# Plain float32 products on half of the array's rows, in a gated causal convolution kernel

## The chip, the core and the metric

One of the eight cores of a Trainium2 chip. The metric is the time of one execution on the device in microseconds (us). The engines: PE multiplies matrices (PEld is its loading of weights), DVE, ACT and POOL work element by element, SP starts transfers, and 16 DMA engines move data. PE writes to PSUM, which ACT and DVE read.

## What is computed

Eight batches of 4224 rows with 192 channels. First a dynamic convolution: each row has, for each of 8 heads of 24 channels, seven weights that a softmax makes, and sums its last seven rows with them. Then a gate: a causal convolution of five taps per channel, a sigmoid, times `x @ w_val`; and the product with `w_out`.

```python
w = np.exp(weight_gen - max) ; w = w / (w.sum(-1) + 1e-9)      # B, S, 8, 7
x = einsum('bshk,bskhg->bshg', w, last seven rows of x)         # dynamic convolution
gate_pre = sum(conv_w[k] * xp[:, k:k + S, :] for k in range(5)) # taps
gate = 1 / (1 + np.exp(-gate_pre))
out = (gate * (x @ w_val)) @ w_out
```

## The kernel before

**Tiling.** A block is 384 rows of one batch (`BLK`), a macro `i` is two blocks, and there are 44 macros. After the dynamic convolution channels lie in partitions and rows along the free dimension. The 192 channels are in two groups. Group A (g = 0) is 128 channels of a block, so a macro has two halves of it: tile `A`, 128 x (2 x 388). Group B (g = 1) is the other 64 channels: of a macro's first block in partitions 0 to 63 and of its second in 64 to 127, tile `B`, 128 x 388. The four extra columns are the history that the taps read.

**Stages of a macro**, each a function with the macro's index:

- `load_x`, `load_t`: SP's transfers of x and of the softmax weights (`tb`, from a scratch `zd` in DRAM that `Softmax.norm` writes through POOL's queue).
- `bank` (L355): four PSUM banks `pa` of 16 products each, in tiles of 32 columns of the array, four side by side.
- `evac` (L393, L395, L399): ACT copies the banks to `A`, `B` and a helper `S`; `moves` then fills holes in A and B from S with small transfers.
- `tap0` on ACT (L421, L424) and `tap` on DVE (L429), four each per group: the causal convolution into `aA` (128 x 768) and `aB` (128 x 384). `sigm` on ACT (L433).
- `split_a` (ACT L440, POOL L441) writes A as the sum of two parts of 12 bits, `hi` and `lo`. `split_b` and `gsplit` use `stack` (ACT L447, POOL L448): it puts the high part of block u's half into its own half of the partitions and the low part into the other half, into `q` (from B) and `g` (from the gated aB).
- `val`, three PSUM banks `pv`: kinds 0 and 1 are the first 128 output channels of block 0 and 1, five products each of float32r parts (L462); kind 2 is the other 64 output channels of both blocks in plain float32: one product on all of B (`wvd`, L464) and two with 64 columns each on A (`wvm`, L466).
- `gv` (DVE L473): gate times val, into aA or aB.
- `omm` (PE, L489, L490, L491): for 128 rows of a block, `g` times `woh`, `g` times `wob[u]` (both float32r, 256 columns), and aA times `woa` in plain float32 (192 columns). Two such chunks make a unit with one PSUM tile `po`, three units a macro.
- `oev` (ACT L499): copies `po` to `ot`; after the last unit SP sends ot to DRAM. The last macro sends each unit by itself.

**Order.** Every engine runs its instructions in the order of emission. `PLAN` gives each stage an offset in macros from its macro's index, and all stages are sorted by index plus offset: the dynamic convolution of macro i comes with val of macro i - 3 and out of macro i - 4 or i - 5. `Softmax` of later batches (max, sub, sum, recip, norm on DVE, exp on ACT) is spread between. PSUM: three tiles for `pa`, three for `pv`, two for `po`. Tiles of `A`, `B` and `S` hold two macros each and have two buffers.

Of the kernel before, what the change touches and what calls it, by code (L numbers as in the profile page):

```python
# [16 lines left out]
# The order in which the parts of the macros' work are emitted: each at the macro's index plus a number from here.  # L17
# [7 lines left out]
    splitB=2.7981,  # L25
    splitA=2.3938,
# [4 lines left out]
    gsplit=3.8257,  # L31
# [8 lines left out]
    spo=(2.2858, 3.439),  # L40
# [14 lines left out]
def tile_dynconv_gated_moe(  # L55
# [9 lines left out]
    nc = tc.nc  # L65
# [45 lines left out]
    wvh = const.tile([P, 2, P], FP32R, name="wvh")  # L111
    wvl = const.tile([P, 2, P], FP32R, name="wvl")
    wvb = [const.tile([P, P], FP32R, name=f"wvb{i}") for i in range(2)]
    wvm = const.tile([P, HD], FP32, name="wvm")
    wvd = const.tile([P, P], FP32, name="wvd")
    WO = 256
    woh = const.tile([P, WO], FP32R, name="woh")
    wob = [const.tile([P, WO], FP32R, name=f"wob{i}") for i in range(2)]
# [9 lines left out]
    woa = wf[:, 0, D:2 * D]  # L128

    # Channels live in two groups of partitions: group 0 is 128 channels of a block, group 1 the other 64,  # L130
    # those of a macro's first block in the lower half, of its second in the upper. Each quadrant holds 24
    # channels of one head and 8 of the last two heads.
# [11 lines left out]
    def order_weights():  # L144
        """Rows of the weights in DRAM in the order of their channels in the partitions."""
        d = wd.rearrange("(q r) n -> q r n", r=Q)
        for rows, c0, n in ((slice(0, C), 0, C), (slice(C, Q), c6, HC)):
            for j, w in enumerate((w_val, w_out)):
                nc.gpsimd.dma_start(out=d[:, rows, j * D:(j + 1) * D],
                                    in_=w[c0:c0 + n * NQ].rearrange("(q r) n -> q r n", r=n))  # L150
            nc.gpsimd.dma_start(out=cd.rearrange("j (q r) -> j q r", r=Q)[:, :, rows],
                                in_=conv_w[:, c0:c0 + n * NQ].rearrange("j (q r) -> j q r", r=n))
# [9 lines left out]
    def convert_weights(raw, cs, v, w):  # L162
        """raw, float64 in pairs of words (low, high), rounded to float32 in columns cs of wf."""
# [19 lines left out]
    def split_weights():  # L183
        """The columns of w_val in the order of the channels in the partitions: towards the first group as sums
        of two parts of 12 bits each, towards the second as they are. The second group's rows of w_out as such
        sums too."""
        units = []

        def runs(dst, src, q0, q1):
            """Quadrants q0 .. q1 - 1 of the columns: (dst, src) for both runs of channels in them."""  # L190
            d = dst.rearrange("p (a c) -> p a c", c=Q)
            return ((d[:, :, 0:C], src[:, C * q0:C * q1].rearrange("p (a c) -> p a c", c=C)),
                    (d[:, :, C:Q], src[:, c6 + HC * q0:c6 + HC * q1].rearrange("p (a c) -> p a c", c=HC)))
# [7 lines left out]
        for g in (1, 0):  # L201
            for (h, v), (l, _) in zip(runs(wvh[:, g], wf[:, g, 0:D], 0, 4), runs(wvl[:, g], wf[:, g, 0:D], 0, 4)):
                units.append(lambda h=h, v=v: nc.scalar.copy(out=h, in_=v))
                units.append(lambda h=h, l=l, v=v: nc.gpsimd.tensor_tensor(
                    out=l, in0=v, in1=h.bitcast(FP32), op=ALU.subtract))
            if g == 1:
                for b in range(2):
                    hs = slice(HD * b, HD * b + HD)
                    units.append(lambda b=b, hs=hs: nc.scalar.copy(out=wvb[b][hs], in_=wvl[hs, 1].bitcast(FP32)))
        s = wf[:, 1, D:2 * D]  # L210
        out_units = [lambda: nc.scalar.copy(out=woh[:, 0:D], in_=s)]
        for b in range(2):
            hs = slice(HD * b, HD * b + HD)
            out_units.append(lambda b=b, hs=hs: nc.gpsimd.tensor_tensor(
                out=wob[b][hs, 0:D], in0=s[hs], in1=woh[hs, 0:D].bitcast(FP32), op=ALU.subtract))
        return units, out_units
# [5 lines left out]
    class Softmax:  # L222
        """Softmax of rows r0 .. r0 + P * R - 1 of batch b: partition p takes R of them and the
        PAD after those, so that norm() can write for an input row its weights towards each output."""
# [72 lines left out]
    def where(i):  # L297
        """The two blocks of macro i as (batch, first row)."""
        return [((2 * i + u) // NBLK, (2 * i + u) % NBLK * BLK) for u in range(2)]

    def parts(i):
        """Runs of windows of macro i that lie at one distance: (batch, first row, window, windows)."""
# [37 lines left out]
    def bank(i, kind):  # L340
        """One PSUM bank of the dynamic convolution of macro i: block 0's or block 1's first four heads, the next
        two heads of both blocks, or the last two of both."""
# [24 lines left out]
    def pair(i, name, shape):  # L367
        """The tile of that name of macros i and i ^ 1."""
# [12 lines left out]
    def stir(n):  # L381
        """Work of no effect that keeps the clock of the tensor engine up while the first loads are on the way."""
# [18 lines left out]
    def moves(i, g):  # L401
        """Fill the holes of macros i - 1 and i, or of i alone where it is the only one left."""
# [32 lines left out]
    def split_a(i):  # L435
        s = st[i]
        a = s["A"][:, :, HALO:W]
        s["hi"] = work.tile([P, 2, BLK], FP32R, name="hi")
        s["lo"] = work.tile([P, 2, BLK], FP32R, name="lo")
        nc.scalar.copy(out=s["hi"], in_=a)  # L440
        nc.gpsimd.tensor_tensor(out=s["lo"], in0=a, in1=s["hi"].bitcast(FP32), op=ALU.subtract)  # L441

    def stack(src, dst, eng):
        """dst[:, u]: the high part of block u's half of src in its own half, the low part in the other."""
        for u in range(2):
            own, oth = slice(HD * u, HD * u + HD), slice(HD - HD * u, P - HD * u)
            nc.scalar.copy(out=dst[own, u], in_=src[own])  # L447
            eng.tensor_tensor(out=dst[oth, u], in0=src[own], in1=dst[own, u].bitcast(FP32), op=ALU.subtract)  # L448

    def split_b(i):  # L450
        s = st[i]
        s["q"] = work.tile([P, 2, BLK], FP32R, name="q")
        stack(s["B"][:, HALO:W], s["q"], nc.gpsimd)

    def val(i, k):
        s = st[i]
        pv = ps_v.tile([P, 512], FP32, name="pv")
        if k < 2:
            ops = [(wvh[:, 1], s["q"][:, k]), (wvb[k], s["q"][:, k]),
                   (wvh[:, 0], s["hi"][:, k]), (wvh[:, 0], s["lo"][:, k]), (wvl[:, 0], s["hi"][:, k])]  # L460
            for n, (w, r) in enumerate(ops):
                nc.tensor.matmul(out=pv[:, 0:BLK], lhsT=w, rhs=r, start=(n == 0), stop=(n == len(ops) - 1))  # L462
        else:
# [4 lines left out]
        s["pv", k] = pv  # L468
# [6 lines left out]
    def gsplit(i):  # L475
        s = st[i]
        s["g"] = work.tile([P, 2, BLK], FP32R, name="g")
        stack(s["aB"], s["g"], nc.gpsimd)

    CPB = BLK // CH  # L480
    OPU = 2

    def omm(i, k):
        s = st[i]
        po = ps_o.tile([P, OPU, WO], FP32, name="po")
        for v in range(OPU):
            u, j = divmod(k * OPU + v, CPB)
            cs = slice(CH * j, CH * j + CH)
            nc.tensor.matmul(out=po[:, v, :], lhsT=s["g"][:, u, cs], rhs=woh, start=True, stop=False)  # L489
            nc.tensor.matmul(out=po[:, v, :], lhsT=s["g"][:, u, cs], rhs=wob[u], start=False, stop=False)  # L490
            nc.tensor.matmul(out=po[:, v, 0:D], lhsT=s["aA"][:, u, cs], rhs=woa, start=False, stop=True)  # L491
        s["po", k] = po

    def oev(i, k):
# [4 lines left out]
        nc.scalar.copy(out=ot[:, k * OPU:(k + 1) * OPU, :], in_=s["po", k][:, :, 0:D])  # L499
        if i == NM - 1 and len(parts(i)) == 1:  # L500
            (b, r, _, _), = parts(i)
            r += k * OPU * CH
            nc.sync.dma_start(out=out[b, r:r + OPU * CH, :].rearrange("(t p) d -> p t d", p=P),
                              in_=ot[:, k * OPU:(k + 1) * OPU, :])
        elif (k + 1) * OPU == 2 * CPB:
# [4 lines left out]
            st[i] = {}  # L510

# [11 lines left out]
    for i in range(NM):  # L523
# [24 lines left out]
        at(sh + i + PLAN["splitB"], split_b, i)  # L548
        at(sh + i + PLAN["splitA"], split_a, i)
        for k, tt in zip((2, 0, 1), span(i, "val", 3)):  # L550
            at(sh + tt, val, i, k)
            at(sh + tt + PLAN["gvlag"], gv, i, k)
        at(sh + i + PLAN["gsplit"], gsplit, i)
        n = 2 * CPB // OPU
        for k, tt in enumerate(span(i, "out", n)):
# [24 lines left out]
    def clear(t, h, eng):  # L580
        """Zero half h of t."""
# [16 lines left out]
    for t in (*wvb, woh, *wob):  # L598
        nc.gpsimd.memset(t.bitcast(FP32), 0.0)
# [29 lines left out]
    sv, so = split_weights()  # L629
    for key, us in (("cvc", conv[2]), ("cvv", conv[0]), ("cvo", conv[1]), ("spv", sv), ("spo", so)):  # L630
# [3 lines left out]
    for _, _, f, a in sorted(ev, key=lambda e: e[:2]):  # L634
        f(*a)

# [25 lines left out]
```

## Time and profile before

| | |
|---|---|
| median of 3 runs | 649.92 us (647.55 to 651.01) |
| the profiled execution, its span | 650.0 us |
| mean granted TensorE clock | 0.971 |
| PE busy | 582.7 us (90%) |
| DVE busy | 601.7 us (93%) |
| ACT busy | 438.0 us (67%) |
| POOL busy | 376.6 us (58%) |
| DMA | 124.65 MB, mean 192 GB/s |

The span runs from the first to the last instruction of the profiled execution; its own time beside the span is not recorded apart, and the span stands within 0.1 us of the median. A row of a group reads: line, engine, operation, tile written <- tiles read, shapes, count, then busy us and mean ns of one, then the idle time of the engine before them and what ended most of it. A row of a timeline reads: start, length (to the end of the last where several are grouped), engine, line, operation, tiles, shapes, count. The length of a product includes its way through the array, so that successive ones overlap; what one costs in a dense run is read from start to start. L numbers are lines of the kernel before.

### The profile page before, as it was taken

How to read it: one execution, taken by the hardware profiler on the slowest of the kernel's cores; microseconds unless marked ns; L12 is line 12 of the kernel's file. 1: busy time of each engine (PE TensorE's matmuls, PEld its weight loads, DVE VectorE, ACT ScalarE, POOL GpSimd, SP SyncE). 2: the span in 40 equal slices, each digit the busy share in tenths (PEclk: the TensorE clock that was granted, in tenths of full speed). 3: DMA queues.
4: the chain of work that ended last, by engine and by line, in shares of the span. 5: the costliest groups of instructions: out<-in, count | busy, mean ns of one | idle time of the engine just before them, and what ended most of it. 6: DMA issues, size and time to landing. Idle time of an engine off the chain costs nothing.

```text
span 650.0 us, 18233 instructions
## 1 busy us (share of the span) xinstructions
PE 582.7 (90%) x7422; PEld 459.1 (71%) x7422; DVE 601.7 (93%) x653; ACT 438.0 (67%) x789; POOL 376.6 (58%) x292
## 2 busy tenths in 40 slices
PE   1356699998998999997999979998998999999976
PEld 0345477876787778775778857787876887788766
DVE  7867999999999899998999989998999998898994
ACT  4436396687748687586776768757966676667763
POOL 9154744774755645572665727556656556455673
PEclk9986799999999999999999999999998999999998
DMA  6879967997896968987598876997878658754313
GB/s 191 225 244 176 315 154 167 282 247 155 176 291 197 203 145 206 295 227 154 125 275 214 224 158 129 247 248 188 197 196 288 156 135 196 168 123 114 86 44 110
DMA packets 126914, 124.65 MB, mean 192 GB/s; under 512 B 9390, under 2 KB 121354, under 8 KB 126062
## 3 DMA queue, kind: packets, MB, share of 16 engines
q1 hardware_dynamic: 122970, 101.25, 65.3%
q0 software_dynamic: 3840, 22.23, 9.2%
q8 instruction: 59, 0.97, 0.7%
q14 instruction: 25, 0.20, 0.1%
q10 hardware_dynamic: 20, 0.01, 0.0%
HBM read 67.12 MB, written 50.36 MB: 181 GB/s over the span
## 4 chain that ended last, share of the span: by engine, by line
PE 45%; DVE 22%; DMA 19%; issue 4%; SPq 4%; ACT 4%; POOL 1%; DVEq 0%; ACTq 0%; POOLq 0%
PE pa L355 21%; DVE aA L429 9%; PE po L491 7%; DVE aB L429 6%; PE pv L462 5%; DMA tb<-zd 4%; DMA A<-S 4%; PE po L489 4%; DMA wt<-in_weight_gen_dram 3%; DMA zd<-zt 3%; PE pv L464 3%; PE pv L466 3%; PE po L490 3%; DVE zt L280 2%; SPq L334 2%
## 5 line engine op out<-in xcount | busy, mean ns | idle before, releaser
L355 PE MATMUL pa<-tb,xt 106*32 106x96 f32 (+1 forms) x5632 | 267.9, 357 | 37.4 <-ACT wt L260 22.2
L355 PEld LDWEIGHTS pa<-tb,xt 106*32 106x32 f32 x5632 | 206.7, 129 | 100.3 <-issue 63.1
L429 DVE SCALAR_TENSOR_TENSOR aA<-A,wf,aA 128x768 f32<-128x768 f32 x176 | 226.2, 1286 | 2.5 <-ACT aA L421 2.5
L429 DVE SCALAR_TENSOR_TENSOR aB<-B,wf,aB 128x384 f32<-128x384 f32 x176 | 193.5, 1100 | 0.0
L448 POOL TENSOR_TENSOR q<-B,q 64x384 fp32r<-64x384 f32 x88 | 112.3, 1277 | 99.6 <-ACT q L447 66.1
L441 POOL TENSOR_TENSOR lo<-A,hi 128x768 fp32r<-128x768 f32 x44 | 93.8, 2132 | 101.9 <-issue 35.2
L448 POOL TENSOR_TENSOR g<-aB,g 64x384 fp32r<-64x384 f32 x88 | 126.6, 1439 | 12.9 <-ACT g L447 6.4
L491 PE MATMUL po<-wf,aA 128*128 128x192 f32 x528 | 131.1, 330 | 2.1 <-DVE aA L473 2.1
L489 PE MATMUL po<-woh,g 128*128 128x256 f32 x264 | 98.9, 374 | 17.6 <-ACT ot L499 12.9
L491 PEld LDWEIGHTS po<-wf,aA 128*128 128x128 f32 x528 | 81.8, 191 | 2.6 <-DVE aA L473 2.5
L499 ACT COPY ot<-po 128x384 f32<-128x384 f32 x132 | 62.7, 476 | 25.2 <-PE po L491 24.2
L489 PEld LDWEIGHTS po<-woh,g 128*128 128x128 f32 x264 | 50.4, 191 | 35.4 <-ACT ot L499 15.2
L490 PE MATMUL po<-wob,g 128*128 128x256 f32 x264 | 74.4, 282 | 0.0
L393 ACT COPY A<-pa 128x388 f32<-128x388 f32 x88 | 41.2, 481 | 46.3 <-PE pa L355 27.5
L399 ACT COPY S<-pa 64x388 f32<-64x388 f32 x88 | 42.2, 479 | 29.9 <-PE pa L355 29.3
L473 DVE TENSOR_TENSOR aA<-pv,aA 128x384 f32<-128x384 f32 x88 | 48.1, 547 | 7.3 <-ACT aA L433 6.3
L490 PEld LDWEIGHTS po<-wob,g 128*128 128x128 f32 x264 | 50.6, 192 | 0.0
L421 ACT ACTIVATE aA<-A,wf 128x768 f32<-128x768 f32 x44 | 41.4, 941 | 12.7 <-DMA A<-S 9.1
L447 ACT CAST g<-aB 64x384 fp32r<-64x384 f32 x88 | 45.0, 512 | 4.6 <-DVE aB L473 2.7
L395 ACT COPY B<-pa 128x388 f32<-128x388 f32 x44 | 21.3, 483 | 38.0 <-DVE aB L429 17.8
L433 ACT ACTIVATE aA<-aA 128x768 f32<-128x768 f32 x44 | 37.4, 851 | 13.6 <-DVE aA L429 13.4
L447 ACT CAST q<-B 64x384 fp32r<-64x384 f32 x88 | 44.5, 506 | 1.1
(74 smaller groups left out, 711.0 us busy)
## 6 DMA issues: line engine op xcount, KB each, us to landing
xt<-in_x_dram SPq DMA_DIRECT2D x35, 672.0 KB
out_dram<-ot SPq DMA_DIRECT2D x39, 576.0 KB
tb<-zd SPq DMA_DIRECT2D x240, 88.0 KB
zd<-zt POOLq DMA_DIRECT2D x21, 968.0 KB, 6.8
wt<-in_weight_gen_dram SPq DMA_DIRECT2D x6, 1092.0 KB
A<-S SPq DMA_DIRECT2D x84, 48.5 KB
xt<-in_x_dram SPq DMA_DIRECT2D x5, 588.0 KB
out_dram<-ot SPq DMA_DIRECT2D x8, 288.0 KB
```

Of the source, the lines that this page charges most:

```text
L355: nc.tensor.matmul(out=pa[Q * c:Q * c + Q, at:at + n], lhsT=xb[0:KR, j, C * h:C * h + Q], rhs=t[0:KR, j, PAD + skip:PAD + skip + n, h], st ...
L399: nc.scalar.copy(out=t[:, 2 * m + u, :], in_=pa[HD * u:HD * u + HD, 0:W])
L421: nc.scalar.activation(out=s["aA"], in_=s["A"][:, :, 0:BLK], func=AF.Copy, scale=cw[:, 0, 0:1])
L429: nc.vector.scalar_tensor_tensor(out=a, in0=src, scalar=cw[:, g, j:j + 1], in1=a, op0=ALU.mult, op1=ALU.add)
L441: nc.gpsimd.tensor_tensor(out=s["lo"], in0=a, in1=s["hi"].bitcast(FP32), op=ALU.subtract)
L447: nc.scalar.copy(out=dst[own, u], in_=src[own])
L448: eng.tensor_tensor(out=dst[oth, u], in0=src[own], in1=dst[own, u].bitcast(FP32), op=ALU.subtract)
L473: nc.vector.tensor_tensor(out=a, in0=s["pv", k][:, 0:BLK], in1=a, op=ALU.mult)
L489: nc.tensor.matmul(out=po[:, v, :], lhsT=s["g"][:, u, cs], rhs=woh, start=True, stop=False)
L490: nc.tensor.matmul(out=po[:, v, :], lhsT=s["g"][:, u, cs], rhs=wob[u], start=False, stop=False)
L491: nc.tensor.matmul(out=po[:, v, 0:D], lhsT=s["aA"][:, u, cs], rhs=woa, start=False, stop=True)
L499: nc.scalar.copy(out=ot[:, k * OPU:(k + 1) * OPU, :], in_=s["po", k][:, :, 0:D])
```

## The change

The splits into 12-bit parts are gone (`split_a`, `split_b`, `gsplit`, `stack`, and the split weights `wvh`, `wvl`, `woh`). `val` of kinds 0 and 1 is emitted as one step: for each block a product on 64 rows of the array (`wvb[hs]` with block u's half of B, `tile_position=(64 * u, 0)`), then for each block one product on all rows (`wva` with A), all in plain float32. `omm` makes two units a macro: chunks 0 and 1 of both blocks, then chunk 2 of both. A unit takes two `po` tiles, one per block; its products of aA come first, then those of aB on half of the rows, alternating between the blocks. `oev` copies the two tiles apart. The last macro's output goes in one transfer. `probe`, emitted last, runs 64 products of no effect on a cleared tile `pz`, in tiles of 32 columns, and four float32r products. The other numbers of `PLAN` stay.

```diff
-    splitB=2.7981,
-    splitA=2.3938,
-    gsplit=3.8257,
-    spo=(2.2858, 3.439),
...
-        pv = ps_v.tile([P, 512], FP32, name="pv")
-        if k < 2:
-            ops = [(wvh[:, 1], s["q"][:, k]), (wvb[k], s["q"][:, k]),
-                   (wvh[:, 0], s["hi"][:, k]), (wvh[:, 0], s["lo"][:, k]), (wvl[:, 0], s["hi"][:, k])]
-            for n, (w, r) in enumerate(ops):
-                nc.tensor.matmul(out=pv[:, 0:BLK], lhsT=w, rhs=r, start=(n == 0), stop=(n == len(ops) - 1))
...
+        for k in kinds:
+            s["pv", k] = ps_v.tile([P, 512], FP32, name="pv")
...
+        for k in kinds:
+            hs = slice(HD * k, HD * k + HD)
+            nc.tensor.matmul(out=s["pv", k][:, 0:BLK], lhsT=wvb[hs], rhs=s["B"][hs, HALO:W], start=True, stop=False,
+                             tile_position=(HD * k, 0))
+        for k in kinds:
+            nc.tensor.matmul(out=s["pv", k][:, 0:BLK], lhsT=wva, rhs=s["A"][:, k, HALO:W], start=False, stop=True)
...
+    OUNITS = ((0, 1), (2,))
     def omm(i, k):
-        po = ps_o.tile([P, OPU, WO], FP32, name="po")
-        for v in range(OPU):
-            u, j = divmod(k * OPU + v, CPB)
-            cs = slice(CH * j, CH * j + CH)
-            nc.tensor.matmul(out=po[:, v, :], lhsT=s["g"][:, u, cs], rhs=woh, start=True, stop=False)
-            nc.tensor.matmul(out=po[:, v, :], lhsT=s["g"][:, u, cs], rhs=wob[u], start=False, stop=False)
-            nc.tensor.matmul(out=po[:, v, 0:D], lhsT=s["aA"][:, u, cs], rhs=woa, start=False, stop=True)
+        po = [ps_o.tile([P, 2, 256], FP32, name="po") for _ in range(2)]
+        for u in range(2):
+            for v, j in enumerate(OUNITS[k]):
+                nc.tensor.matmul(out=po[u][:, v, 0:D], lhsT=s["aA"][:, u, CH * j:CH * j + CH], rhs=woa, start=(v == 0),
+                                 stop=False, skip_group_check=True)
+        for v, j in enumerate(OUNITS[k]):
+            for u in range(2):
+                hs = slice(HD * u, HD * u + HD)
+                nc.tensor.matmul(out=po[u][:, v, 0:D], lhsT=s["aB"][hs, CH * j:CH * j + CH], rhs=wob[hs], start=False,
+                                 stop=True, skip_group_check=True, tile_position=(HD * u, 0))
...
-        nc.scalar.copy(out=ot[:, k * OPU:(k + 1) * OPU, :], in_=s["po", k][:, :, 0:D])
+        for u in range(2):
+            nc.scalar.copy(out=ot[:, CPB * u + j:CPB * u + j + n, :], in_=s["po", k][u][:, 0:n, 0:D])
...
+        tv = span(i, "val", 3)
+        at(sh + tv[0], val, i, (2,))
+        at(sh + tv[1], val, i, (0, 1))
...
     for _, _, f, a in sorted(ev, key=lambda e: e[:2]):
         f(*a)
+    probe()
```

More of the change, by code (lines that the diff above doesn't have):

```diff
@@ L110, in tile_dynconv_gated_moe @@
     xt = [const.tile([P, TW, XC], FP32, name=f"xt{i}") for i in range(3)]
-    wvh = const.tile([P, 2, P], FP32R, name="wvh")
-    wvl = const.tile([P, 2, P], FP32R, name="wvl")
-    wvb = [const.tile([P, P], FP32R, name=f"wvb{i}") for i in range(2)]
+    wva = const.tile([P, P], FP32, name="wva")
+    wvb = const.tile([P, P], FP32, name="wvb")
     wvm = const.tile([P, HD], FP32, name="wvm")
     wvd = const.tile([P, P], FP32, name="wvd")
-    WO = 256
-    woh = const.tile([P, WO], FP32R, name="woh")
-    wob = [const.tile([P, WO], FP32R, name=f"wob{i}") for i in range(2)]
+    pz = const.tile([P, 800], FP32, name="pz")
     zero = const.tile([P, PITCH], FP32, name="zero")
@@ L128, in tile_dynconv_gated_moe @@
     woa = wf[:, 0, D:2 * D]
+    wob = wf[:, 1, D:2 * D]
     c6, c7, HC = C * NQ, C * (NQ + 1), Q - C
@@ L200, in split_weights @@
                 units.append(lambda d=d, v=v: nc.scalar.copy(out=d, in_=v))
[L201 to L216, printed above, removed]
+        for d, v in runs(wvb, wf[:, 1, 0:D], 0, 4):
+            units.append(lambda d=d, v=v: nc.scalar.copy(out=d, in_=v))
+        for d, v in runs(wva, wf[:, 0, 0:D], 0, 4):
+            units.append(lambda d=d, v=v: nc.scalar.copy(out=d, in_=v))
+        return units
     ROW = H * K
@@ L433, in sigm, with val @@
         nc.scalar.activation(out=a, in_=a, func=AF.Sigmoid)
-    def split_a(i):
+    def val(i, kinds):
         s = st[i]
[L437 to L456, printed above, removed]
-        pv = ps_v.tile([P, 512], FP32, name="pv")
-        if k < 2:
-            ops = [(wvh[:, 1], s["q"][:, k]), (wvb[k], s["q"][:, k]),
-                   (wvh[:, 0], s["hi"][:, k]), (wvh[:, 0], s["lo"][:, k]), (wvl[:, 0], s["hi"][:, k])]
-            for n, (w, r) in enumerate(ops):
-                nc.tensor.matmul(out=pv[:, 0:BLK], lhsT=w, rhs=r, start=(n == 0), stop=(n == len(ops) - 1))
-        else:
+        for k in kinds:
+            s["pv", k] = ps_v.tile([P, 512], FP32, name="pv")
+        if kinds == (2,):
+            pv = s["pv", 2]
             nc.tensor.matmul(out=pv[:, 0:BLK], lhsT=wvd, rhs=s["B"][:, HALO:W], start=True, stop=False)
@@ L467, in val @@
                                  stop=True, tile_position=(0, HD * u))
-        s["pv", k] = pv
+            return
+        for k in kinds:
[4 more added lines that the diff above has]
+            nc.tensor.matmul(out=s["pv", k][:, 0:BLK], lhsT=wva, rhs=s["A"][:, k, HALO:W], start=False, stop=True)
     def gv(i, k):
@@ L473, in gv @@
         nc.vector.tensor_tensor(out=a, in0=s["pv", k][:, 0:BLK], in1=a, op=ALU.mult)
[L475 to L478, printed above, removed]
     CPB = BLK // CH
-    OPU = 2
+    OUNITS = ((0, 1), (2,))
     def omm(i, k):
         s = st[i]
-        po = ps_o.tile([P, OPU, WO], FP32, name="po")
-        for v in range(OPU):
-            u, j = divmod(k * OPU + v, CPB)
-            cs = slice(CH * j, CH * j + CH)
-            nc.tensor.matmul(out=po[:, v, :], lhsT=s["g"][:, u, cs], rhs=woh, start=True, stop=False)
-            nc.tensor.matmul(out=po[:, v, :], lhsT=s["g"][:, u, cs], rhs=wob[u], start=False, stop=False)
-            nc.tensor.matmul(out=po[:, v, 0:D], lhsT=s["aA"][:, u, cs], rhs=woa, start=False, stop=True)
+        po = [ps_o.tile([P, 2, 256], FP32, name="po") for _ in range(2)]
[8 more added lines that the diff above has]
+                                 stop=True, skip_group_check=True, tile_position=(HD * u, 0))
         s["po", k] = po
@@ L498, in oev @@
         ot = s["ot"]
[L499 to L505, printed above, removed]
+        j, n = OUNITS[k][0], len(OUNITS[k])
+        for u in range(2):
+            nc.scalar.copy(out=ot[:, CPB * u + j:CPB * u + j + n, :], in_=s["po", k][u][:, 0:n, 0:D])
+        if k + 1 == len(OUNITS):
             for b, r, w0, nw in parts(i):
@@ L510, in oev, with probe, four @@
             st[i] = {}
+    def probe():
+        def four(rhs, n):
+            for _ in range(4):
+                pa = ps_a.tile([P, 512], FP32, name="pa")
+                for c in range(4):
+                    nc.tensor.matmul(out=pa[Q * c:Q * c + Q, 0:n], lhsT=pz[0:106, 0:Q], rhs=rhs, start=True, stop=True,
+                                     tile_position=(0, Q * c))
+        z = pz[0:106]
+        four(z[:, 0:96], 96)
+        four(z[:, 0:768].rearrange("p (a b) -> p a b", b=16)[:, :, 0:2], 96)
+        four(z[:, 0:192].rearrange("p (a b) -> p a b", b=2)[:, :, 0], 96)
+        four(z[:, 0:122], 122)
+        for _ in range(4):
+            pv = ps_v.tile([P, 512], FP32, name="pv")
+            nc.tensor.matmul(out=pv[:, 0:D], lhsT=pz.bitcast(FP32R)[:, 0:P], rhs=pz.bitcast(FP32R)[:, 0:D], start=True, stop=True)
     ev = []
@@ L547, in tile_dynconv_gated_moe @@
             at(sh + i + PLAN["sig" + n], sigm, i, g)
[L548 to L551, printed above, removed]
+        tv = span(i, "val", 3)
+        at(sh + tv[0], val, i, (2,))
+        at(sh + tv[1], val, i, (0, 1))
+        for k, tt in zip((2, 0, 1), tv):
             at(sh + tt + PLAN["gvlag"], gv, i, k)
-        at(sh + i + PLAN["gsplit"], gsplit, i)
-        n = 2 * CPB // OPU
-        for k, tt in enumerate(span(i, "out", n)):
+        for k, tt in enumerate(span(i, "out", len(OUNITS))):
             at(sh + tt, omm, i, k)
@@ L597, in tile_dynconv_gated_moe @@
     nc.gpsimd.memset(wvd, 0.0)
-    for t in (*wvb, woh, *wob):
-        nc.gpsimd.memset(t.bitcast(FP32), 0.0)
+    nc.gpsimd.memset(pz, 0.0)
     f0.max(0)
@@ L628, in tile_dynconv_gated_moe @@
     conv = [convert_weights(raw[:, :, c], c, nc.vector, nc.gpsimd if k < 2 else nc.vector) for k, c in enumerate(cs)]
-    sv, so = split_weights()
-    for key, us in (("cvc", conv[2]), ("cvv", conv[0]), ("cvo", conv[1]), ("spv", sv), ("spo", so)):
+    for key, us in (("cvc", conv[2]), ("cvv", conv[0]), ("cvo", conv[1]), ("spv", split_weights())):
         lo, hi = PLAN[key]
```

## Prediction

> **What bounds the kernel now.** I read the totals first, then busy time by stretch, then the PE timeline of one undisturbed macro, then what runs beside the slow DVE instructions, and last the chain of waits where PE stands still.
>
> ```profile
> PE 582.7 (90%) x7422; PEld 459.1 (71%) x7422; DVE 601.7 (93%) x653; ACT 438.0 (67%) x789; POOL 376.6 (58%) x292
> ```
> ```profile
> 26.00:103.30 77.30, 58.92 (x884) 45.98 (x884) 66.09 (x88) 44.94 (x85) 38.82 (x33) 0.85 0.82 209
> 103.30:601.30 498.00, 481.59 (x6220) 379.60 (x6219) 477.10 (x510) 353.61 (x647) 292.99 (x211) 0.99 0.79 198
> ...
> 608.90:650.00 41.10, 31.45 (x182) 26.92 (x178) 31.21 (x32) 23.04 (x43) 22.69 (x17) 0.96 0.26 78
> ```
>
> The columns of the second fence are the stretch, its length, busy PE, PE weight load, DVE, ACT and POOL, the granted clock, the DMA share and GB/s. Macro 6 starts its dynamic convolution at 103.3 us and macro 43, the last, at 601.3, so the long row is 37 macros of 13.46 us. Both PE and DVE are busy 96% of it at a full clock. Totals can't say which of them binds; one macro on PE can:
>
> ```profile
> 510.95 0.37 PE L355 MATMUL pa<-tb,xt 106*32 106x100 f32 x4
> 513.93 0.91 PE L464 MATMUL pv<-B,wvd 128*128 128x384 f32 x2
> 514.36 0.49 PE L464 MATMUL pv<-B,wvd 128*128 128x384 f32 x1
> 514.78 0.54 PE L466 MATMUL pv<-A,wvm 128*64 128x384 f32 x2
> 515.15 0.49 PE L466 MATMUL pv<-A,wvm 128*64 128x384 f32 x2
> 515.57 0.35 PE L355 MATMUL pa<-tb,xt 106*32 106x100 f32 x1
> 518.55 0.38 PE L489 MATMUL po<-woh,g 128*128 128x256 f32 x1
> 518.77 0.28 PE L490 MATMUL po<-wob,g 128*128 128x256 f32 x1
> 519.64 0.47 PE L462 MATMUL pv<-q,wvh 128*128 128x384 f32 x1
> 520.65 0.28 PE L489 MATMUL po<-woh,g 128*128 128x256 f32 x1
> 520.77 0.28 PE L490 MATMUL po<-wob,g 128*128 128x256 f32 x1
> 520.89 0.48 PE L491 MATMUL po<-wf,aA 128*128 128x192 f32 x2
> 521.33 0.28 PE L490 MATMUL po<-wob,g 128*128 128x256 f32 x1
> 523.86 0.37 PE L355 MATMUL pa<-tb,xt 106*32 106x100 f32 x4
> ```
>
> From 510.95 to 523.86 PE goes through one macro without a gap: 12.91 us. It spends 2.98 on two banks of the dynamic convolution, 1.64 on the val of the third bank (L464, L466), 2.98 on two more banks, and 5.31 (518.55 to 523.86) on the val and out products that the change rewrites. So PE binds wherever nothing else disturbs it, and the 37 macros hold 498.0 - 37 x 12.91 = 20.3 us of disturbance. What disturbs is seen on DVE:
>
> ```profile
> 208.35 0.60 DVE L429 SCALAR_TENSOR_TENSOR aB<-B,wf,aB 128x384 f32<-128x384 f32 x1
> 208.88 1.01 DVE L429 SCALAR_TENSOR_TENSOR aA<-A,wf,aA 128x768 f32<-128x768 f32 x1
> ...
> 211.09 1.77 DVE L429 SCALAR_TENSOR_TENSOR aA<-A,wf,aA 128x768 f32<-128x768 f32 x1
> 212.79 1.37 DVE L429 SCALAR_TENSOR_TENSOR aB<-B,wf,aB 128x384 f32<-128x384 f32 x1
> ```
> ```profile
> 209.13 2.92 POOL L448 TENSOR_TENSOR q<-B,q 64x384 fp32r<-64x384 f32 x2 [2.51 <-ACT q L447]
> 212.12 2.90 POOL L448 TENSOR_TENSOR g<-aB,g 64x384 fp32r<-64x384 f32 x2
> ```
> ```profile
> L429 DVE SCALAR_TENSOR_TENSOR aA<-A,wf,aA 128x768 f32<-128x768 f32 x176 | 226.2, 1286 | 2.5 <-ACT aA L421 2.5
> L429 DVE SCALAR_TENSOR_TENSOR aB<-B,wf,aB 128x384 f32<-128x384 f32 x176 | 193.5, 1100 | 0.0
> ...
> L448 POOL TENSOR_TENSOR q<-B,q 64x384 fp32r<-64x384 f32 x88 | 112.3, 1277 | 99.6 <-ACT q L447 66.1
> L441 POOL TENSOR_TENSOR lo<-A,hi 128x768 fp32r<-128x768 f32 x44 | 93.8, 2132 | 101.9 <-issue 35.2
> L448 POOL TENSOR_TENSOR g<-aB,g 64x384 fp32r<-64x384 f32 x88 | 126.6, 1439 | 12.9 <-ACT g L447 6.4
> L491 PE MATMUL po<-wf,aA 128*128 128x192 f32 x528 | 131.1, 330 | 2.1 <-DVE aA L473 2.1
> ```
>
> The same tap takes 0.60 us (384 elements) or 1.01 (768) while POOL is still, and 1.37 or 1.77 while a POOL subtraction runs. The means over all 176, 1.100 and 1.286, sit between. The Trainium skill (GPSIMD Engine Reference, its table of specifications) says that GpSimd's SBUF interfaces are shared with VectorE, with contention for DVE instructions that have two SBUF inputs; the trace agrees with 0.60 against 1.37 us. A late tap stops PE by this route:
>
> ```profile
> 193.32 2.27 DVE aA L429
> ...
> 195.67 0.87 ACT A L393 x2
> 196.53 0.39 ACT ot L499
> ...
> 196.97 0.39 PE po L489
> ```
>
> ACT may not refill a buffer of A before DVE's last tap has read it; the output copy (`ot`) queues behind that on ACT, and PE's next out product waits for the copy. The waits put 12.9 us in six stalls on that last step:
>
> ```profile
> PE po L489 <- ACT ot L499: 12.9, 6, 4.1
> PE po L489 <- POOL g L448: 4.7, 3, 3.0
> PE pv L464 <- DVE aB L473: 3.6, 2, 3.0
> ```
>
> **The change, part by part.** *Splitting goes.* All of L440, L441, L447 and L448 go: 332.7 us of POOL (112.3 + 93.8 + 126.6) and five ACT casts per macro. The output copies become four per macro (two of 384, two of 192 elements) in place of three. Neither engine binds, so their time is worth nothing by itself. What counts is DVE: 176 x (1.286 - 1.01) + 176 x (1.100 - 0.60) = 137 us, 3.1 us per macro. DVE in the long stretch is 477.1/37 = 12.9 us per macro, as long as PE's; after, 9.8. The cover that hid any slip in DVE was nothing; now it is over 3 us per macro. Of the 20.3 us of disturbance I keep 5, for stalls that start with late DMAs (share 0.79): **-15 us**, bounds -20 and -5.
>
> *PE, passes.* A plain float32 product leaves two records (528 for the 264 of L491), each a pass. From L490 to the next L490 is 0.56 us, L489 and L490 take 0.12 each, so a pass of 192 columns costs 0.16 and one of 384 costs 0.32. Changes of tile shape show at L464/L466: the second pass of L464 starts at 514.36, would end 0.32 later, and the next shape starts at 514.78: 0.10 of draining. The first pass of L464 holds 0.43 - 0.32 = 0.11 of loading 128 columns of weights. A change towards 128 columns so costs 0.21.
>
> *PE, do two half-row products run at once?* No row shows products on 64 rows. The nearest are L466's, on 64 columns: their two products, four passes, take 0.79 us from 514.78 to 515.57, both first passes before 515.15, and one after the other they would need 4 x 0.32 = 1.28 and more. They run side by side, so I take the half-row pairs as side by side too.
>
> *PE, the sum per macro.* In the emitted order: weights 0.11; four woa products 1.28; change 0.21; two wob pairs 0.64; the wvb pair 0.64 in the same shape; change 0.21; two wva products 1.28; two woa 0.64; change 0.21; one wob pair 0.32; drain 0.10. That is 5.64 against 5.31: **+0.33 us per macro**, 13.24 in all, +12 us over the 37. Bounds: if changes between whole and half rows cost nothing, 5.0; if pairs run one after the other, 5.64 + 0.64 + 3 x 0.32 = 7.24. The Trainium skill (TensorEngine Tiling (Array Packing), Key Properties) says that changing the tiling mode drains TensorE; by it the three changes are due, as I charge them, and without it the sum would be 5.0.
>
> *New waits.* `omm` takes both po buffers at once, so the second unit waits for both copies of the first. Between the two lies `val` with 2.1 us, and the copies need 0.87 at most (two as L393's): hidden, unless ACT is held by an exp with its table load, queued ahead of it. Both blocks' last gv now precede the first out product; DVE's slack covers it.
>
> *Start.* PE waited for DVE's gv there (the 3.6 us row); less contention gives back up to 4 us, the added passes of three macros take 1: **-2**, bounds -5 and +1.
>
> *Tail.*
>
> ```profile
> 608.89 0.38 PE L489 MATMUL po<-woh,g 128*128 128x256 f32 x1
> ...
> 645.88 0.49 PE L491 MATMUL po<-wf,aA 128*128 128x192 f32 x2
> ```
> ```profile
> 646.40 0.48 ACT L499 COPY ot<-po 128x384 f32<-128x384 f32 x1 [0.64 <-PE po L491]
> ```
>
> The last bank is done at 608.9; 41.1 us follow with DVE busy 31.2 and PE 31.45. Some 21 taps (12 long, 9 short) fall to 12 x 1.01 + 9 x 0.60 = 17.5 us, nine less than they take now, and the waits for POOL's `g` (4.7 us) go. PE's own work, a microsecond or two longer, then binds: **-6**, bounds -10 and -2. The tiles that POOL clears at the start swap nearly like for like (1024 columns of wvb, woh and wob for 800 of pz).
>
> *End.* After its last product PE now runs the 64 products of `probe`, as many as a macro's dynamic convolution (32 took 2.98 us): at most 6 us, and the four at the end some 0.5. They lie beside the last copy and the output DMA, which took 650.0 - 646.4 = 3.6 us and is now one transfer instead of three. **+2**, bounds 0 and +3.
>
> Sum: 650.0 + 12 - 15 - 2 - 6 + 2 = 641 against the profiled execution, whose span of 650.0 is the median of the three runs (649.92). I predict **641 us**.
>
> **The rivals.** *Half-row pairs run one after the other* (the other side). Place: the four pairs of each macro; price 1.60 us each macro, 44 x 1.6 = 70, giving 711. It turns to slower once less than about 80% of the overlap happens (0.2 x 70 = 14 us). For it: no row shows row tiles. Against it: L466.
>
> *Pairs overlap, their weights don't.* Each wob pass of a pair then needs 2 x 0.11 = 0.22 of loading in place of 0.16: six passes, 0.36, and two first loads of 0.11 more: 0.58 per macro, 44 x 0.58 = 26, giving 667. Against it: L466's loads overlap, but those are short (64 columns), so this says little. The Trainium skill (TensorE: Matmul & The Clock Gate, Measured speedup vs the span model) gives 3.07 for four row tiles where four would be perfect; an estimate by that ratio, 1.60/0.77, adds 0.48 per macro and gives 662.
>
> *Shape changes between whole and half rows are free*: 37 x 0.63 less, 618 to 625. For it: neither changes the columns. Against it: both changes at L464 and L466 drained.
>
> *The stalls stay*, because transfers and not DVE cause them (DMA share 0.79): 641 + 15 = 656.
>
> **How the numbers follow.** Forecast 0.57, its own range 628 to 652; pairs in sequence 0.15; weights in sequence or partial overlap 0.15; free changes 0.07; stalls stay 0.06. A measurement tells 0.5% (3.2 us) from no change. Faster: 0.50 of the forecast and the free changes, 0.57. Same: 0.07 of the forecast and a third of the stalls, 0.09 with rounding. Slower: the rest, 0.34. The range leaves out the sequence case and a little at both ends: 624 to 670.
>
> **What would show it.** Right: L440, L441, L447, L448 gone; all taps near 0.60 and 1.01; DVE near 465 us busy (601.7 - 137); a macro period near 13.2 with hardly a gap; both products of a wvb pair starting within 0.05 us. Wrong: the second product of a pair starting 0.65 us after the first, a period of 13.8 or 14.8, PE waiting for `ot` at the second out unit, or a tail still near 41 us.

## The result, and the profile after

The changed kernel takes 693.99 us (median of four runs, 691.16 to 695.94) beside 650.46 for the kernel before on the same chip: 1.0658 times as long, 95% interval 1.0612 to 1.0703. The profiled execution has a span of 692.7 us. The forecast was 641 us. Two of the experiments below had one slow run each, of 823 and 815 us, which their medians leave out.

The totals come first: busy us, share of the span and instructions of each engine of the changed kernel. From here on L numbers are lines of the kernel whose view it is. In the changed kernel L336 is the dynamic convolution, L376, L374 and L380 are ACT's copies to B, A and S, L410 is the taps, L424, L426, L431 and L434 are `val`, L439 is the gate product, L450 and L455 are `omm`, and L466 is the copy to `ot`.

```profile
PE 608.8 (88%) x7466; PEld 404.4 (58%) x7466; DVE 449.5 (65%) x653; ACT 317.0 (46%) x610; POOL 40.5 (6%) x62
```

POOL and ACT lost what they should (376.6 to 40.5, 438.0 to 317.0), and DVE fell by 152 us. Only PE is busier than before (608.8, was 582.7), and it now has holes. The stretches, with the same columns as in the prediction, from the first bank of macro 6 to that of macro 43, and from there to the end:

```profile
110.74:646.06 535.32, 499.04 (x6144) 330.06 (x6143) 345.87 (x505) 250.06 (x493) 11.12 (x24) 0.99 0.74 184
646.06:692.70 46.64, 43.06 (x438) 28.34 (x436) 27.20 (x42) 18.61 (x41) 0.00 (x0) 1.00 0.27 84
```

Against the kernel before, macro 6 starts 7.4 us later (110.74, was 103.34), the 37 macros take 37.3 us more (535.3, was 498.0), and from macro 43's start to the end it is 2.1 us less (46.6, was 48.7). So the loss lies in the macros. PE's timeline of one macro that runs without a gap, and the start of the macro before it in the first row:

```profile
546.18 0.37 PE L336 MATMUL pa<-tb,xt 106*32 106x100 f32 x4
...
561.24 3.03 PE L336 MATMUL pa<-tb,xt 106*32 106x100 f32 x64
...
568.79 1.57 PE L450 MATMUL po<-wf,aA 128*128 128x192 f32 x8
570.29 0.92 PE L455 MATMUL po<-wf,aB 64*128 64x192 f32 x8
571.04 0.81 PE L431 MATMUL pv<-B,wvb 64*128 64x384 f32 x4
571.79 1.56 PE L434 MATMUL pv<-A,wva 128*128 128x384 f32 x4
573.18 0.81 PE L450 MATMUL po<-wf,aA 128*128 128x192 f32 x4
573.92 0.59 PE L455 MATMUL po<-wf,aB 64*128 64x192 f32 x4
574.45 0.90 PE L336 MATMUL pa<-tb,xt 106*32 106x100 f32 x16
```

This macro takes 13.21 us (561.24 to 574.45), the one before it 15.06 (546.18 to 561.24). So it goes on: from macro 6 to 42 every even one takes 15.1 us (19.1 and 19.2 at macros 20 and 26), the odd ones 13.2 to 13.8. PE's stretch from the out products to the next bank (568.79 to 574.45) takes 5.66 us without waiting. In the slow macros one hole stands behind `val`:

```profile
352.10 0.92 PE L455 MATMUL po<-wf,aB 64*128 64x192 f32 x8
352.86 0.81 PE L431 MATMUL pv<-B,wvb 64*128 64x384 f32 x4
353.60 1.56 PE L434 MATMUL pv<-A,wva 128*128 128x384 f32 x4
356.68 0.97 PE L450 MATMUL po<-wf,aA 128*128 128x192 f32 x4 [1.52 <-ACT ot L466]
```

PE waits for the output copies of the unit before. ACT's timeline of the same microseconds says why these are late:

```profile
344.73 0.97 ACT L380 COPY S<-pa 64x388 f32<-64x388 f32 x2 [0.52 <-PE pa L336]
353.76 0.48 ACT L376 COPY B<-pa 128x388 f32<-128x388 f32 x1 [8.06 <-issue]
354.14 0.94 ACT L402 ACTIVATE aA<-A,wf 128x768 f32<-128x768 f32 x1
354.98 0.51 ACT L414 ACTIVATE aB<-aB 128x384 f32<-128x384 f32 x1
355.39 0.85 ACT L374 COPY A<-pa 128x388 f32<-128x388 f32 x2
356.12 0.88 ACT L466 COPY ot<-po 128x384 f32<-128x384 f32 x2
```

ACT stands still for 8.06 us in front of its copy into B, and starts it at 353.76, just after PE's products on B (L431) are through (352.86 to 353.67). Then it works off what has piled up, and `ot` comes fifth. "issue" means that the trace shows no releaser; that it is L431 is read from the times here, and tested below. The sums over the whole execution:

```profile
ACT B L376 <- issue: 153.4, 19, 8.1
...
PE po L450 <- ACT ot L466: 38.3, 22, 4.8
```

### The profile page after: what moved, and what is told of

The parts are those of the page before. It is cut to its first block, busy times and chain, and to the rows that moved or that the text cites. A ratio compares the mean times of both kernels' runs of the same rounds, so it can differ in the third digit from the quotient of the medians.

```text
span 692.7 us, 17842 instructions
## 1 busy us (share of the span) xinstructions
PE 608.8 (88%) x7466; PEld 404.4 (58%) x7466; DVE 449.5 (65%) x653; ACT 317.0 (46%) x610; POOL 40.5 (6%) x62
## 4 chain that ended last, share of the span: by engine, by line
PE 72%; issue 10%; DMA 6%; DVE 6%; ACT 5%; SPq 1%; POOL 0%; DVEq 0%; POOLq 0%; ACTq 0%
PE pa L336 30%; PE po L450 13%; PE pv L434 8%; PE po L455 8%; PE pv L424 5%; PE pv L426 4%; PE pv L431 4%; DMA zd<-zt 2%; ACT A L374 2%; DMA tb<-zd 1%; DVE aA L410 1%; DVE mx L232 1%; SPq L315 1%; ACT aB L414 1%; DMA B<-S 1%
## 5 line engine op out<-in xcount | busy, mean ns | idle before, releaser
L336 PE MATMUL pa<-tb,xt 106*32 106x96 f32 (+1 forms) x5632 | 266.8, 357 | 35.6 <-DMA tb<-zd 33.6
L336 PEld LDWEIGHTS pa<-tb,xt 106*32 106x32 f32 x5632 | 202.7, 129 | 102.2 <-issue 67.8
L410 DVE SCALAR_TENSOR_TENSOR aA<-A,wf,aA 128x768 f32<-128x768 f32 x176 | 177.8, 1011 | 7.8 <-ACT aA L402 7.8
L450 PE MATMUL po<-wf,aA 128*128 128x192 f32 x528 | 111.3, 346 | 39.1 <-ACT ot L466 38.3
L450 PEld LDWEIGHTS po<-wf,aA 128*128 128x128 f32 x528 | 85.7, 191 | 76.1 <-ACT ot L466 50.9
L439 DVE TENSOR_TENSOR aB<-pv,aB 128x384 f32<-128x384 f32 x44 | 24.5, 556 | 144.8 <-ACT aB L414 143.2
L410 DVE SCALAR_TENSOR_TENSOR aB<-B,wf,aB 128x384 f32<-128x384 f32 x176 | 106.1, 603 | 5.8 <-ACT aB L405 5.6
L466 ACT COPY ot<-po 128x192 f32<-128x192 f32 (+1 forms) x176 | 62.0, 407 | 85.0 <-PE po L455 73.9
L376 ACT COPY B<-pa 128x388 f32<-128x388 f32 x44 | 21.2, 483 | 164.6 <-issue 153.4
L439 DVE TENSOR_TENSOR aA<-pv,aA 128x384 f32<-128x384 f32 x88 | 48.6, 553 | 43.9 <-ACT aA L414 42.8
L434 PE MATMUL pv<-A,wva 128*128 128x384 f32 x176 | 69.9, 521 | 0.0
L455 PE MATMUL po<-wf,aB 64*128 64x192 f32 x528 | 68.3, 364 | 0.0
L374 ACT COPY A<-pa 128x388 f32<-128x388 f32 x88 | 40.5, 482 | 51.0 <-PE pa L336 50.8
L380 ACT COPY S<-pa 64x388 f32<-64x388 f32 x88 | 42.2, 480 | 43.1 <-PE pa L336 42.6
L455 PEld LDWEIGHTS po<-wf,aB 64*128 64x128 f32 x528 | 41.7, 189 | 20.4 <-issue 20.4
L434 PEld LDWEIGHTS pv<-A,wva 128*128 128x128 f32 x176 | 30.3, 192 | 36.5 <-issue 25.1
L431 PE MATMUL pv<-B,wvb 64*128 64x384 f32 x176 | 37.7, 490 | 5.6 <-DVE aA L439 5.6
L424 PE MATMUL pv<-B,wvd 128*128 128x384 f32 x88 | 41.6, 555 | 0.0
L426 PE MATMUL pv<-A,wvm 128*64 128x384 f32 x176 | 38.2, 513 | 0.0
L261 DVE TENSOR_TENSOR zt<-wt,mx 128x616 f32<-128x616 f32 (+2 forms) x25 | 30.9, 1237 | 7.6 <-DMA zd<-zt 7.6
```

Source lines behind the costliest of these rows:

```text
L336: nc.tensor.matmul(out=pa[Q * c:Q * c + Q, at:at + n], lhsT=xb[0:KR, j, C * h:C * h + Q], rhs=t[0:KR, j, PAD + skip:PAD + skip + n, h], st ...
L374: nc.scalar.copy(out=pair(i, "A", [P, 4, W])[:, 2 * m + kind, :], in_=pa[:, 0:W])
L410: nc.vector.scalar_tensor_tensor(out=a, in0=src, scalar=cw[:, g, j:j + 1], in1=a, op0=ALU.mult, op1=ALU.add)
L424: nc.tensor.matmul(out=pv[:, 0:BLK], lhsT=wvd, rhs=s["B"][:, HALO:W], start=True, stop=False)
L426: nc.tensor.matmul(out=pv[HD * u:HD * u + HD, 0:BLK], lhsT=wvm, rhs=s["A"][:, u, HALO:W], start=False, stop=True, tile_position=(0, HD * u))
L431: nc.tensor.matmul(out=s["pv", k][:, 0:BLK], lhsT=wvb[hs], rhs=s["B"][hs, HALO:W], start=True, stop=False, tile_position=(HD * k, 0))
```

## The experiments

All times are medians; "37 macros" is from macro 6's first bank to macro 43's, "disturbance" what they hold above 37 undisturbed periods. An undisturbed period is 12.91 us in the kernel before and 13.24 in the changed one. The theory came out of PLAN, once the trace had pointed there. A tile of B holds two macros and has two buffers, so the pair that starts with macro m + 3 reuses the buffer whose last reader is `val` of macro m (m odd). That `val` is emitted at m + 3.57, the copy into B at m + 3.25 in ACT's order: the copy must wait for PE to come to a step that stands 0.32 macros later. Before the change the last readers of B were the splits (2.8), the taps (3.00) and kind 2 (3.19), all ahead of the copy. Of A, one tap (3.47) already stood behind ACT's copy (3.41): the route by which a late tap stopped PE.

**Three buffers for A and B.**

```diff
...
-                t = work.tile([P, 4 * W + 4], FP32, name=name)
+                t = work.tile([P, 4 * W + 4], FP32, name=name, bufs=3)
...
-                pairs[k] = work.tile(shape, FP32, name=name)
+                pairs[k] = work.tile(shape, FP32, name=name, bufs=3 if name == "B" else 2)
```

> The changed kernel with three buffers in place of two for the tiles A and B. Theory (lifetime): val of both blocks now reads B and A itself, on PE at offset 3.57, where the splits had read them at 2.4 to 2.8; so ACT's copy into B of the first macro of a pair has to wait for the val of a macro three before, ACT stands still some 8 us, the output copies behind it come late, and PE stops 1.85 us every second macro. With a third buffer the wait is gone: all macros at 13.2 us except a few, 22 stalls of PE on the output copies (38.3 us) down to under 8 us, time about 655 (694 - 38). Rival (po): PE stops because a unit of out takes both po tiles, whatever ACT's copies into A and B do; then the period stays alternating 13.2 and 15.1 and the time stays within 2 us of 694.

Measured: 647.3 us, ratio to the kernel before 0.9946 (0.9926 to 0.9966). Its 37 macros and its two waits of these kinds:

```profile
107.32:598.90 491.58, 490.25 (x6143) 331.42 (x6142) 350.27 (x508) 254.57 (x493) 11.11 (x24) 1.00 0.80 201
```
```profile
ACT B L376 <- PE pa L336: 19.4, 43, 0.7
```
```profile
PE po L450 <- ACT ot L466: 3.3, 4, 1.7
```

The period is 13.21 to 13.35 in all macros but two (14.31 at macro 7, 14.08 at macro 20), the disturbance 1.7 us, and ACT's copies wait only for the bank that they copy. This one edit takes off 46.7 us, more than the 43.5 that the change had cost; the theory holds, and that a unit of out takes both po tiles costs at most the 3.3 us of that last row.

**A third buffer for B alone, and for A alone.**

> The changed kernel with three buffers for B alone, A stays at two. Theory (lifetime): the copy into B is free, but the first copy into A, which stands later in ACT's order, still waits for the last product of the same val, 1.4 us later on PE than the products on B. ACT is then released later but has less to do (two copies into A and one output copy, about 1.2 us, in place of 3.0 us): the stall of every second macro goes from about 1.85 to about 1.3 us, time about 682 (686 to 676). If only B mattered, it would be near 655. Rival (po): no change, 694.

> The changed kernel with three buffers for A alone, B stays at two. Theory (lifetime): ACT's copy into B, which stands first in its order, waits for the val product on B as before, and the copies into A behind it had nothing left to wait for by then; so nothing is gained: alternating 13.2 and 15.1, 690 to 694. If A were the one that counts, 650 to 660.

Measured: 688.95 us with B alone (ratio 1.0594, 1.0565 to 1.0624), 694.03 with A alone (1.0663, 1.0632 to 1.0694). A alone does nothing, as expected. B alone does nearly nothing, and I had expected 682: the slow macros take 14.97 us where 15.06 were. The wait moves to the copy into A, and ACT is released too late all the same.

```profile
ACT A L374 <- issue: 94.5, 14, 7.4
...
ACT A L374 <- PE pv L434: 35.8, 5, 7.4
```

Here the trace names the releaser in five of the cases: L434, the product of `val` on A. Either tile alone is enough for the stall; both must go.

**Without the products at the end.** The call of `probe` is left out.

> The changed kernel without the 68 products of no effect at its end. The prediction had +2 us for the end, bounds 0 and +3. In the changed kernel's trace the products run 3.8 us from 686.3 to 690.1, and the last output copy ends at 686.95. If the end of the span hangs on them, the time falls by 1 to 2.5 us; if it hangs on the one large output transfer, it does not fall (within 0.5).

Measured: 691.04 us (ratio 1.063, 1.0585 to 1.0674), beside 1.0658 with them; the intervals overlap. From the start of macro 43 to the end it is 45.5 us (688.5 - 643.0) instead of 46.6, so about 1 us goes there. The rest is not told apart from the scatter of the start.

**The kernel before without POOL's subtractions.**

```diff
...
-        s["lo"] = work.tile([P, 2, BLK], FP32R, name="lo")
+        s["lo"] = lo0
...
-        nc.gpsimd.tensor_tensor(out=s["lo"], in0=a, in1=s["hi"].bitcast(FP32), op=ALU.subtract)
...
-            eng.tensor_tensor(out=dst[oth, u], in0=src[own], in1=dst[own, u].bitcast(FP32), op=ALU.subtract)
...
```

The low parts now lie in tiles that POOL clears once at the start; `q` and `g` take turns between two such tiles each.

> The kernel before with the POOL subtractions of the splits left out: all low parts are zero throughout (written once at the start), so the products see the high parts alone; PE, ACT and DVE issue the same instructions. It measures the term of -15 us, what POOL's running beside DVE costs the kernel before. Theory of the prediction: the taps fall to 1.0 and 0.6 us, the 20.3 us of disturbance in the 37 macros fall to about 5, the tail loses some 6 us (with the waits for g), the time is about 627 to 632. Rival: transfers and exp cause the disturbance, not DVE: the taps are as short, but 15 us or more of disturbance stay and the time is 640 to 648.

Measured: 623.3 us, ratio 0.9604 (0.9555 to 0.9654).

```profile
101.71:580.60 478.89, 477.45 (x6217) 378.95 (x6216) 351.51 (x508) 353.74 (x647) 11.13 (x24) 1.00 0.82 206
580.60:620.90 40.30, 36.59 (x313) 30.52 (x312) 25.02 (x38) 27.44 (x52) 0.00 (x0) 1.00 0.33 97
```

The disturbance falls from 20.3 to 1.2 us, the end from 48.7 to 40.3. So in the kernel before, POOL's subtractions cost 27 us, more than the forecast's 15 and 6. That is the late taps and the waits for the subtractions' own results (4.7 us of PE's for `g`) together; the run does not part them. The stalls were not the transfers': the DMA share is 0.82 here and was 0.79.

**POOL's subtractions put back into the kernel with three buffers**, from A, B and aB, into tiles that nothing reads.

> As the kernel with three buffers for A and B, with five POOL subtractions per macro of the old sizes put back at their old places, from A, B and aB into tiles that nothing reads. Theory (contention): the taps go back to means near 1.1 and 1.29, DVE to 12.9 us per macro against PE's 13.24; disturbance grows from 1.5 to 8 to 15 us and the tail by some 8: 661 to 670. Rival: the third buffer takes up a late DVE, the 37 macros stay within 3 us, only the tail grows: 653 to 657.

Measured: 653.72 us (ratio to the kernel before 1.0058, 1.003 to 1.0085), 6.4 more than without them. The rival holds.

```profile
108.54:598.05 489.51, 489.51 (x6143) 331.44 (x6142) 426.60 (x507) 254.85 (x493) 256.68 (x212) 1.00 0.82 201
598.05:651.60 53.55, 45.90 (x438) 30.11 (x436) 32.67 (x40) 18.70 (x41) 17.91 (x14) 0.93 0.25 73
```

DVE is 76 us longer in the 37 macros (426.6, was 350.3), and they don't move (489.5, was 491.6); the end pays all of it (53.6, was 46.7). The taps' means are 1.229 and 0.836 us, less than the 1.29 and 1.1 expected, but far above 1.01 and 0.60.

**Three buffers for A and B in the kernel before.**

> The kernel before with three buffers for A and B and nothing else changed in its work (to make room, three small tiles that only the start uses share the space of later ones). With the subtractions put back into the changed kernel, the 37 macros did not move although the taps were slow. Theory: a late tap costs PE time only because ACT's copy into A or B waits for it; with a third buffer the 20.2 us of disturbance fall below 5 and the time is 632 to 638; the tail, where DVE works off its queue, stays near 48 us. Rival: DVE at 12.9 us per macro is itself a bound in the macros with softmax, so a buffer only delays the stall: 10 us or more of disturbance stay, 640 to 650.

Measured: 642.53 us, ratio 0.9883 (0.9853 to 0.9913): 1.2% faster, with all its splits. The rival was nearer: 11.7 us of disturbance stay above this kernel's period of 12.86 (9.8 above 12.91). PE's waits for `ot` are down to 2.6 us, but others remain that no buffer of A or B removes, 5.2 us for the gate product and 4.8 for `g` behind it:

```profile
PE po L495 <- DVE aA L477: 5.2, 5, 2.2
...
PE po L493 <- POOL g L452: 4.8, 4, 2.6
PE po L493 <- ACT ot L503: 2.6, 4, 1.5
```

This run is also the fair partner of the changed kernel with three buffers, and that one is slower, 647.3 against 642.53 us. Its 37 macros save 10 us of disturbance (11.7 to 1.7) and pay 0.38 us of period each, 14 us: 491.6 us against 487.5.

**The start.** PE's rows of the changed kernel around 73 us:

```profile
72.99 0.91 PE L431 MATMUL pv<-B,wvb 64*128 64x384 f32 x2 [0.15 <-DVE aA L439]
79.30 1.65 PE L431 MATMUL pv<-B,wvb 64*128 64x384 f32 x2 [5.40 <-DVE aA L439]
80.88 2.93 PE L434 MATMUL pv<-A,wva 128*128 128x384 f32 x4
83.73 0.57 PE L336 MATMUL pa<-tb,xt 106*32 106x100 f32 x8
```

The second product waits for a PSUM tile that a gate product of the macro before must read, then runs slowly (the four L434 take 2.93 us here and 1.56 later): the granted clock is 0.50 from 79 to 84 us. Macro 4's dynamic convolution starts at 83.73; in the kernel before it was 79.26. The experiment, on the kernel with three buffers:

```diff
-        at(sh + tv[1], val, i, (0, 1))
+        if i < 4:
+            at(sh + tv[1], val, i, (0,))
+            at(sh + tv[2], val, i, (1,))
+        else:
+            at(sh + tv[1], val, i, (0, 1))
```

> As the kernel with three buffers for A and B, but the val of block 0 and block 1 of macros 0 to 3 are emitted as two steps again, each at its old place. Theory: val of both blocks at once needs two PSUM tiles at once, so PE waits for the second gate product of the macro before (5.4 us at 73.9 in the changed kernel) with the dynamic convolution of macro 4 queued behind it. Apart, macro 4 starts some 4 us earlier and macro 6 at 103 to 104 instead of 107.3; time 643 to 644 (3 to 4 us less). Rival: the start hangs on transfers (tb from zd, 31.7 us of PE's waits), and nothing moves by more than 1 us.

Measured: 641.75 us (ratio 0.9864, 0.9819 to 0.9909), 5.6 less; macro 6 starts at 101.4 instead of 107.3. (Over the seven profiled executions with `val` of both blocks at once, macro 6 starts at 106.6 to 110.7.) PE's wait shrinks to one of 1.36 us, and the granted clock from 69 to 80 us is 1.00:

```profile
72.90 0.91 PE L431 MATMUL pv<-B,wvb 64*128 64x384 f32 x2 [1.36 <-DVE aA L439]
73.74 0.91 PE L434 MATMUL pv<-A,wva 128*128 128x384 f32 x2
74.58 1.62 PE L336 MATMUL pa<-tb,xt 106*32 106x100 f32 x32
```

**The half-row products apart.**

```diff
         for k in kinds:
             ... wvb[hs] ...
-        for k in kinds:
             ... wva ...
```

> As the kernel with three buffers for A and B, but val takes block 0's half-row product, block 0's product on all rows, then the same for block 1, so that the two half-row products can't run side by side and two more shape changes stand between. From the rows: 0.64 for the lost overlap and 2 x 0.21 for the changes, 1.06 per macro: a period of 14.30 in place of 13.24, and about 690 (44 x 1.06 more, less what the waits at the end take up). If changes between half and whole rows were free, 13.9 and 675.

Measured: 688.99 us (ratio 1.0567, 1.0528 to 1.0607), 41.7 more than in pairs.

```profile
405.70 0.80 PE L431 MATMUL pv<-B,wvb 64*128 64x384 f32 x2
406.44 0.91 PE L433 MATMUL pv<-A,wva 128*128 128x384 f32 x2
407.28 0.91 PE L431 MATMUL pv<-B,wvb 64*128 64x384 f32 x2
408.12 0.91 PE L433 MATMUL pv<-A,wva 128*128 128x384 f32 x2
408.87 0.81 PE L449 MATMUL po<-wf,aA 128*128 128x192 f32 x4
```

The period is 14.26, 1.02 more; 1.06 was forecast. From start to start `val` takes 3.17 us (405.70 to 408.87) where in pairs it takes 2.14 (571.04 to 573.18).

**The version that the runs point to**: three buffers, the start apart, no products at the end, the last macro's output in four transfers.

> As the one with the start apart, without the 68 products at the end, and with the last macro's output in four transfers, each right behind its copy, instead of one. By the run without these products (about 2 us) and by the size of the last transfer (192 instead of 576 KB) the end loses 2 to 3.5 us: 640 to 642, 1.4% below the kernel before. If the span hangs on the copy's way to DRAM alone, 643.

Measured: 638.75 us (638.13 to 639.44), ratio to the kernel before 0.9804 (0.9778 to 0.9831). From macro 43's start to the end 43.9 us instead of 46.8. It beats both kernels. It also beats the kernel before with three buffers (642.53), which has `val` apart at the start, sends its last macro in parts and has no products at its end: by 0.6%. By these two runs, that is what the change itself is worth once its own stalls are undone.

## Why the prediction was wrong

The step that failed is "New waits". It looked at the one buffer that the diff shows, po, and not at the buffers that lose an early reader: A and B. Their readers moved from the splits at 2.4 and 2.8 to `val` at 3.57, behind ACT's next copies at 3.25 and 3.41 in the pair that reuses them. All of these numbers follow from PLAN, and that tiles hold two macros and have two buffers stood in the code. The forecast kept 5 us of disturbance where the trace has 45.4 (535.3 - 37 x 13.24). The sign that the prediction named for this, PE waiting for `ot` at the second out unit, did appear (1.52 us at 356.68), and its condition, that ACT is held, was met; but what held ACT was its own wait for a buffer, and not an exp. Only in macros 20 and 26 did an exp add to it: a table load and an exp, 1.28 and 2.02 us from 323.55 on in macro 20, stand between the late copies and `ot`, and these macros take 4 us more than the other even ones.

By its terms, against the trace:

| term | forecast | measured in the changed kernel | with three buffers |
|---|---|---|---|
| PE's products per macro | +0.33, 13.24 in all | 13.21 to 13.24 where undisturbed | 13.24 |
| disturbance in 37 macros | 20.3 to 5 | 45.4 | 1.7 |
| start, to macro 6 | -2 | +7.4 | +4.0 |
| macro 43 to the end | -6 + 2 | -2.1 | -2.0 |

The sum starts from a span. In all runs that have both on record the time is 1.7 to 1.9 us longer than the span, so the 650.0 of the profiled execution belongs to a time near 652, and 641 to one near 643. That changes nothing in the account.

*PE's sum* was right, part by part: 1.50, 0.75, 0.75, 1.39, 0.74 and 0.53 us from start to start in the timeline, 5.66 against 5.64 forecast. Half-row products do run side by side, and drains are paid at each change; both rivals on that point, and the one with free changes, are out. The Trainium skill's ratio (TensorE: Matmul & The Clock Gate, Measured speedup vs the span model), by which I had estimated 662, doesn't show here: the four passes of a wvb pair take 0.75 us, two passes of 0.32 and a drain of 0.10. Its rule that a changed tiling mode drains (TensorEngine Tiling (Array Packing), Key Properties) does, with that 0.10.

*DVE's relief* came as forecast (taps at 1.011 and 0.603 us, 449.5 us busy where 465 was forecast), and in the kernel before it was worth more than I gave it. But it could not show while ACT stood still; and a third buffer takes half of the disturbance off the kernel before (20.3 to 9.8 above 12.91) without the change.

*The start* failed for a second reason: I priced the added passes and not that `val` of both blocks now asks for two PSUM tiles at one point of PE's order, so that everything queued behind it waits for the later of two gate products. The experiment with the start apart gives 5.6 us back. The +7.4 of the table is one execution; the changed kernel without the products at its end, with the same start, has +4.1 (107.4).

*The tail* was out by 2 us: PE's own work bound it, as written, but the waits for `ot` between the last units (0.40 and 0.61 us) and the end of the products of no effect add to it. Without these products the stretch is 45.5 us: some 1 us of the +2 was theirs, and the -6 was -3.3.

The time fell between two rivals' times by accident; neither mechanism took place. The slower side had 0.34, all for reasons that did not occur.

## What to carry to other kernels

When a change moves the last reader of a tile, compare its place in the order with that of the write that reuses the buffer, in the writer's own queue: a writer that stands ahead of the reader of another engine stops everything behind it. When two steps are joined, count the buffers that the joined step needs at one point, since what is queued behind waits for the last of them. Slack decides what a slow engine costs: POOL's subtractions cost 19 us in the macros of the kernel before (498.0 against 478.9); with a third buffer these macros still took 8.6 us more than without the subtractions (487.5); and put beside the macros of the changed kernel with three buffers they cost nothing. Before a change is credited with removing a stall, ask whether a buffer alone would remove it.

## What the runs showed of the hardware that was not expected

Two products on the two halves of the rows start together (both between 571.04 and 571.05) and cost as one: four passes of 384 columns in 0.75 us from start to start (571.04 to 571.79), which includes 0.10 of draining. Their loads of 128 columns overlap too: with 192 columns a pair's two passes still follow at 0.16 us (eight passes in 0.75, 0.11 of it the first load). And a change between half and whole rows drains as one between column shapes does: taking them apart cost 1.02 us for the lost 0.64 and two changes, 0.19 each.
